# Splitting of the dense network's weights begun one attention step later, with the same order of steps

## The chip, the cores and the metric

The kernel runs on one core of a Trainium2 chip. The metric is the device time of one execution in microseconds (us), the median of three runs. The engines are named PE (matrix multiply; PEld is its weight load), DVE (vector), ACT (scalar), POOL (GpSimd) and SP, which here only issues transfers.

## The reference

Three stages follow one another: windowed attention with some global queries, a dense two-layer network, and a routed network with eight experts. Cut to its core:

```
out_g = softmax(scale * q_g @ k_all.T) @ v_all            # 32 global queries a head
out_l = softmax(mask(scale * q_l @ [k_g, k_l].T)) @ [v_g, v_l]   # |distance| <= 32
x = concat(out_g, out_l) as [1088, 512]
g = maximum(x @ w_in, 0) ** 2                             # w_in 512x2048, float64
x = g @ w_out                                             # w_out 2048x512, float64
e, gate = argmax(softmax(x @ w_gate)), its probability
out = gate * (maximum(x @ w1[e], 0) @ w2[e])              # 8 experts, with a capacity
```

## The kernel before

Attention works on 8 pairs of heads and batches. A loop over `u` from 0 to 20 runs it as a software pipeline; I call one pass an attention step, and `u4` is the pass with u = 4. A string, `ORDER`, sets what a step issues: the scores of half a pair (`S0`, `S1`: products on PE at L123, the mask and a running minimum on DVE at L127, the exponential on ACT at L130), the normalisation of the step before (`N`: DVE L134 and L135, POOL L138 and L140), the transposes of step u-2 (`T`: PE L147 and L151, copied out by DVE L148 and ACT L152), the products with the values of step u-3 (`V0`, `V1`: PE L165 and L168) and their copy (`X`: ACT L175). Every fourth step adds the global queries: `GS` (PE L186, L189) and `GX` at u = 3, 7, 11, 15; `GN` (DVE L206 to L208), `GT` (PE L215, L218; DVE L219; ACT L216) and `GV` (PE L232) in the three steps after. Every engine runs its instructions in the order in which they were written, so an instruction that waits holds up all behind it.

The keys `kd`, queries `qb` and values `vw` of a pair come by transfers that SP issues in the order of the strings `START` and `NEXT`, at the end (`L`) of every second step. The global queries `qg` of the second batch are issued behind the pair loads of u9 and are first read by `GS` at u11. SP too issues in order, and each issue can wait: for a buffer that is still in use, and for an earlier transfer that used the same completion counter.

The dense network's weights are float64. They are cut into 16 units (two halves of each 512-row or 512-column piece; 1 MB each). A unit is loaded into one of three buffers `ws` (SP, L315) and is then split on the core into two fp32r tiles in five steps: `last` (DVE L359), `sign` (DVE L364), `rebase` (ACT L367), `clamp` (DVE L372) and `join` (DVE L375). What is left of a unit rides in the steps of the next: its `high` (ACT L336, whi) in that unit's `sign`, and its `low` (DVE L339, wlo) in that unit's `rebase`, directly followed by the load of a further unit into the buffer that has come free. So units 0, 1 and 2 are loaded by the strings, and the load of unit 3 hangs on step 8 of the whole sequence, unit 4 on step 13, unit 5 on step 18, unit 6 on step 23, unit 7 on step 28.

In attention the table `EARLY` says, for each u, how many of these steps are run at five fillers, `f0` to `f4`, of `ORDER`: it places 28 steps, by ones, at `f0` (behind `N`) and `f2` (behind `S1`). The other 52 follow in the dense network, at the rate that the tables `RATE` set. That network then works in three chunks of tokens (512, 256, 320): L533 to L535 and L553 to L555 on PE, its inputs x split by ACT L511 and DVE L514. The experts come last.

Of the kernel before, what the change touches and what calls it, by code (L numbers as in the profile page):

```python
# [28 lines left out]

SPLIT = [s for u in (16, 17, 18, 19) for s in ((u, 4), (u + 1, 2))]  # L30

EARLY = [[0] * 5] * 2 + [[1, 0, 1, 0, 0]] * 12 + [[0, 0, 1, 0, 0]] * 4 + [[0] * 5] * 4
RATE = [[2, 2]] * 8 + [[2, 3]] * 4 + [[0, 0]] * 4
RATE2 = [[0, 0]] * 8 + [[2, 3], [2, 2]] * 4
NST = 3
# [369 lines left out]
def attention_moe_kernel(ctx, tc, qb, kd, vw, qg, vg, w_in, w_out, w_gate, w_gate_t, w1, w2, capacity, out):  # L405
# [24 lines left out]
    def filler(u, part):  # L430
        if u < 0:
            W.prefetch(part)
        else:
            W.run(EARLY[u][part])
        for v, p in SPLIT:
# [684 lines left out]
```

## Time and profile before

| | us |
|---|---|
| median of 3 runs (lowest to highest) | 465.28 (464.47 to 466.68) |
| the profiled execution | 462.7 |
| span of its trace | 461.0 |
| first product of attention / of the dense network on PE | 3.86 / 85.56 |
| clock of PE, mean granted | 0.988 |

The trace shows one execution. Its times count from the start of its span; 1.7 us of the profiled execution's time lie outside the span. The granted clock of PE is given as a share of 2.4 GHz, so 0.50 is the level of 1.2 GHz.

### The profile page before, as it was taken

To read this page: it belongs to the slowest core of one execution; us is meant where nothing else is said; L and a number is where in the kernel's file an instruction comes from. 1 tells how busy PE (TensorE), PEld (TensorE's weight loads), DVE (VectorE), ACT (ScalarE), POOL (GpSimd) and SP (SyncE) were. 2 spreads that over 40 slices of the span, in tenths; PEclk is the share of its full clock that TensorE was granted. 3 is DMA by queue.
4 is the path that set the end of the run, shared out by engine and by line. 5 is a ranking of instruction groups with operands and counts; after the bars stand their busy time and mean duration, and the time that the engine had idled before them with its cause. 6 is when DMAs were issued, how large, how long until landed. Compare 5 with 4: busy or idle time off the path is not lost. (4 is left out here: it accounts for less than half of the span.)

```text
span 461.0 us, 8010 instructions
## 1 busy us (share of the span) xinstructions
PE 432.4 (94%) x2963; PEld 368.8 (80%) x2963; DVE 315.8 (69%) x690; ACT 249.1 (54%) x488; POOL 79.4 (17%) x106
## 2 busy tenths in 40 slices
PE   5799999999999999999999999799999999999992
PEld 4677777888887889899999999677787777877970
DVE  3598987588799627974598688466974888647200
ACT  4587876576777734222533393156755777356210
POOL 3265636000000000000000000403202512051010
PEclk9899999999999999999999999899999999999998
DMA  8958952325254421005010468485992899711010
GB/s 250 399 182 316 326 196 94 96 91 182 97 186 176 169 104 48 24 1 194 25 46 1 146 254 332 122 257 208 306 305 95 309 349 366 298 52 41 1 39 21
DMA packets 24601, 77.26 MB, mean 168 GB/s; under 512 B 3689, under 2 KB 4841, under 8 KB 24288
## 3 DMA queue, kind: packets, MB, share of 16 engines
q1 hardware_dynamic: 19456, 64.38, 38.7%
q0 software_dynamic: 2384, 6.78, 4.9%
q10 hardware_dynamic: 2704, 5.37, 3.2%
q8 instruction: 32, 0.52, 0.5%
q14 instruction: 25, 0.20, 0.1%
HBM read 70.08 MB, written 7.41 MB: 168 GB/s over the span
## 5 line engine op out<-in xcount | busy, mean ns | idle before, releaser
L339 DVE TENSOR_TENSOR wlo<-ws,whi 128x1024 fp32r<-128x1024 f32 x80 | 94.6, 1219 | 11.5 <-ACT whi L336 10.5
L336 ACT CAST whi<-ws 128x1024 fp32r<-128x1024 f32 x80 | 83.0, 1075 | 19.2 <-DVE ws L375 10.3
L554 PE MATMUL y<-gl,whi 128*128 128x512 f32 (+2 forms) x192 | 63.2, 329 | 1.6 <-DVE gl L545 1.6
L533 PE MATMUL h<-xh,whi 128*128 128x512 f32 (+2 forms) x192 | 63.8, 332 | 0.6 <-ACT r L539 0.6
L535 PE MATMUL h<-xh,wlo 128*128 128x512 f32 (+2 forms) x192 | 62.9, 328 | 0.2 <-DVE wlo L339 0.2
L553 PE MATMUL y<-gh,whi 128*128 128x512 f32 (+2 forms) x192 | 62.9, 327 | 0.0
L534 PE MATMUL h<-xl,whi 128*128 128x512 f32 (+2 forms) x192 | 62.8, 327 | 0.0
L555 PE MATMUL y<-gh,wlo 128*128 128x512 f32 (+2 forms) x192 | 62.8, 327 | 0.0
L539 ACT ACTIVATE r<-h 128x512 f32<-128x512 f32 (+2 forms) x48 | 22.5, 470 | 42.8 <-PE h L535 35.7
L554 PEld LDWEIGHTS y<-gl,whi 128*128 128x128 f32 x192 | 36.3, 189 | 4.8 <-DVE gl L545 2.3
L533 PEld LDWEIGHTS h<-xh,whi 128*128 128x128 f32 x192 | 36.3, 189 | 3.4 <-ACT r L539 0.9
L535 PEld LDWEIGHTS h<-xh,wlo 128*128 128x128 f32 x192 | 36.3, 189 | 3.1 <-DVE wlo L339 0.6
L534 PEld LDWEIGHTS h<-xl,whi 128*128 128x128 f32 x192 | 36.3, 189 | 2.5
L545 DVE TENSOR_TENSOR gl<-r,gh 128x512 fp32r<-128x512 f32 (+2 forms) x48 | 25.7, 536 | 18.4 <-ACT r L542 15.5
L553 PEld LDWEIGHTS y<-gh,whi 128*128 128x128 f32 x192 | 36.3, 189 | 2.5
L555 PEld LDWEIGHTS y<-gh,wlo 128*128 128x128 f32 x192 | 36.3, 189 | 2.5
L130 ACT ACTIVATE P<-P,mn 128x160 f32<-128x160 f32 x64 | 27.0, 427 | 16.4 <-DVE mn L127 14.1
L583 DVE CUSTOM_DVE_ANT_0 junk<-yr,ws 128x512 bf16<-128x512 f32 x48 | 33.1, 690 | 1.2
L123 PE MATMUL s<-kd,qb 128*128 128x160 f32 x128 | 26.7, 343 | 5.2 <-DMA qb<-qb 5.2
L904 PE MATMUL bank_o<-whi,hh 128*128 128x512 f32 x72 | 29.9, 415 | 0.0
L870 POOL DMA_INDIRECT out_dram<-os,sidx x11 | 12.6, 1145 | 97.1 <-ACT os L866 96.5
L905 PE MATMUL bank_o<-wlo,hh 128*128 128x512 f32 x72 | 28.3, 393 | 0.0
(205 smaller groups left out, 895.0 us busy)
## 6 DMA issues: line engine op xcount, KB each, us to landing
ws<-w SPq DMA_DIRECT2D x62, 512.0 KB
ws<-w_in SPq DMA_DIRECT2D x8, 1024.0 KB
ws<-w_out SPq DMA_DIRECT2D x8, 1024.0 KB
vw<-vw SPq DMA_DIRECT2D x8, 512.0 KB
qb<-qb SPq DMA_DIRECT2D x7, 512.0 KB
kd<-kd SPq DMA_DIRECT2D x7, 416.0 KB
ws<-w_gate_t SPq DMA_DIRECT2D x2, 1024.0 KB
out_dram<-yr ACTq DMA_DIRECT2D x1, 2048.0 KB
```

Source lines behind the costliest of these rows:

```text
L130: nc.scalar.activation(out=P[:, a], in_=P[:, a], func=AF.Exp, bias=mn[:, a:a + 1], scale=-1.0, accum_out=su[:, a:a + 1])
L336: self.nc.scalar.copy(d["h"], f)
L339: self.nc.vector.tensor_tensor(out=d["l"], in0=f, in1=d["h"].bitcast(F32), op=ALU.subtract)
L533: nc.tensor.matmul(h, lhsT=whi[:, k, fs], rhs=xh[k], start=(k == 0), stop=False)
L534: nc.tensor.matmul(h, lhsT=whi[:, k, fs], rhs=xl[k], start=False, stop=False)
L535: nc.tensor.matmul(h, lhsT=wlo[:, k, fs], rhs=xh[k], start=False, stop=(k == 3))
L553: nc.tensor.matmul(ys[d][:, 0:gh.shape[1]], lhsT=whi[:, f % 4, ds_], rhs=gh, start=(f == 0), stop=False)
L554: nc.tensor.matmul(ys[d][:, 0:gh.shape[1]], lhsT=whi[:, f % 4, ds_], rhs=gl, start=False, stop=False)
L555: nc.tensor.matmul(ys[d][:, 0:gh.shape[1]], lhsT=wlo[:, f % 4, ds_], rhs=gh, start=False, stop=(f == 15))
L583: nc.vector.tensor_tensor_reduce(out=junk, in0=yr, in1=wgb[e], scale=1.0, scalar=0.0, op0=ALU.mult, op1=ALU.add, accum_out=L[:, i, e:e + 1])
L904: nc.tensor.matmul(o, lhsT=hh[:, k], rhs=wh[:, k % 4], start=(k == 0), stop=False)
L905: nc.tensor.matmul(o, lhsT=hh[:, k], rhs=wl[:, k % 4], start=False, stop=False)
```

## The change

```
-EARLY = [[0] * 5] * 2 + [[1, 0, 1, 0, 0]] * 12 + [[0, 0, 1, 0, 0]] * 4 + [[0] * 5] * 4
+EARLY = [[0] * 5] * 3 + [[1, 0, 1, 0, 0]] * 12 + [[0, 0, 1, 0, 0]] * 4 + [[0] * 5] * 3
```

The two splitting steps of u2 to u13, and the one of u14 to u17, become those of u3 to u14 and u15 to u18. The 28 steps, their order and the fillers within an attention step stay, and so does all that is issued after attention. Loads of units move with the steps that issue them.

DVE at u2, before (su is the softmax sum, tp the transposed weights in PSUM, PT their copy, ws a unit's buffer, s the scores):

```order
L134 TENSOR_SCALAR su<-su 128x4
L135 RECIPROCAL su<-su 128x4
L359 TENSOR_SCALAR ws<-ws 128x1024
L148 COPY PT<-tp_239 128x128
L127 ISA P,mn<-s,mask 128x160
```

The same place now:

```order
L134 TENSOR_SCALAR su<-su 128x4
L135 RECIPROCAL su<-su 128x4
L148 COPY PT<-tp_238 128x128
L127 ISA P,mn<-s,mask 128x160
L127 ISA mn 128x1
```

And DVE one step on, at u3, now:

```order
L134 TENSOR_SCALAR su<-su 128x4
L135 RECIPROCAL su<-su 128x4
L359 TENSOR_SCALAR ws<-ws 128x1024
L148 COPY PT<-tp_282 128x128
L127 ISA P,mn<-s,mask 128x160
```

The first touch of unit 0, L359, has moved from ahead of u2's copy and second scores to ahead of u3's.

SP from the loads of u3 on (- is before, + is now): kd, qb and vw are a pair's keys, queries and values, ws<-w_out is unit 3.

```order
 L75 DMA qb<-qb 128x1024
 L80 DMA vw<-vw 128x1024
-L315 DMA ws<-w_out 128x2x1024
 L74 DMA kd<-kd 128x832
 L75 DMA qb<-qb 128x1024
 L80 DMA vw<-vw 128x1024
+L315 DMA ws<-w_out 128x2x1024
 L74 DMA kd<-kd 128x832
 L75 DMA qb<-qb 128x1024
```

The load of unit 3 has moved from ahead of the loads of pair 4 to behind them. The loads of units 4 and 5 keep their places among SP's issues; that of unit 6 moves behind the last values.

DVE at u8, before, where ws_212 is the buffer of unit 1, which the load of unit 4 takes over:

```order
L134 TENSOR_SCALAR su_544<-su_544 128x4
L135 RECIPROCAL su_544<-su_544 128x4
L339 TENSOR_TENSOR wlo_408<-ws_212,whi_407 128x1024
L206 SCALAR_TENSOR_TENSOR nbg_596<-sg__597 128x1
L207 RECIPROCAL nbg_596<-nbg_596 128x1
L208 TENSOR_SCALAR Pg_588<-Pg_588,nbg_596 128x544
L148 COPY PT_659<-tp2_660 128x128
```

DVE now, from the end of u8 to u9:

```order
L364 SCALAR_TENSOR_TENSOR ws_323<-ws_323 128x1024
L127 ISA P_681,mn_682<-s_684,mask_133 128x160
L127 ISA mn_682 128x1
L127 ISA P_681,mn_682<-s_684,mask_133 128x160
L127 ISA mn_682 128x1
L134 TENSOR_SCALAR su_625<-su_625 128x4
L135 RECIPROCAL su_625<-su_625 128x4
L339 TENSOR_TENSOR wlo_476<-ws_212,whi_475 128x1024
L148 COPY PT_711<-tp2_712 128x128
```

The last reader of unit 1's buffer has moved from `f0` of u8 to `f0` of u9, and with it the moment from which SP may issue the load of unit 4.

## Rows read from the trace of the kernel before

**Rows 1.** Windows view: stretch; length, busy us (instructions) of PE, PEld, DVE, ACT, POOL; PE's clock, DMA share, GB/s.

```profile
22.35:40.61 18.26, 17.62 (x238) 14.19 (x234) 16.25 (x61) 14.60 (x48) 11.55 (x12) 1.00 0.70 268
...
88.00:160.00 72.00, 71.79 (x317) 59.12 (x316) 61.02 (x71) 49.03 (x64) 0.00 (x0) 1.00 0.40 137
```

**Rows 2.** Timeline of DVE at u2: start, duration, engine, line, [idle before, releaser].

```profile
15.59 0.69 DVE L359 TENSOR_SCALAR ws<-ws 128x1024 int32<-128x1024 int32 x1 [3.22 <-DMA ws<-w_in]
16.20 0.28 DVE L148 COPY PT<-tp 128x128 f32<-128x128 f32 x1
```

**Rows 3.** Timeline of PE from u3 to u4.

```profile
13.87 0.34 PE L165 MATMUL o<-PT,vw 128*64 128x64 f32 x4
...
16.54 0.48 PE L168 MATMUL o<-PT,vgz 128*64 128x64 f32 x4 [2.34 <-DVE PT L148]
...
19.54 1.88 PE L186 MATMUL sg<-kd,qg 128*128 128x512 f32 x4
...
22.35 0.81 PE L123 MATMUL s<-kd,qb 128*128 128x160 f32 x4
23.09 0.34 PE L165 MATMUL o<-PT,vw 128*64 128x64 f32 x4
23.26 0.29 PE L168 MATMUL o<-PT,vgz 128*64 128x64 f32 x4
...
24.95 0.34 PE L165 MATMUL o<-PT,vw 128*64 128x64 f32 x4
```

**Rows 4.** Windows view at u2 to u4, columns as in rows 1.

```profile
12.66:16.07 3.41, 1.54 (x14) 1.23 (x12) 0.48 (x1) 0.73 (x3) 1.40 (x3) 1.00 1.04 410
16.08:19.48 3.40, 2.94 (x21) 2.82 (x22) 2.95 (x14) 1.97 (x9) 0.45 (x2) 0.50 1.03 411
...
15.60:22.30 6.70, 5.76 (x45) 4.60 (x45) 5.51 (x22) 4.20 (x14) 1.54 (x3) 0.75 1.02 408
```

**Rows 5.** Page, DMA issues: number of issues and KB of each.

```profile
ws<-w_in SPq DMA_DIRECT2D x8, 1024.0 KB
...
vw<-vw SPq DMA_DIRECT2D x8, 512.0 KB
qb<-qb SPq DMA_DIRECT2D x7, 512.0 KB
kd<-kd SPq DMA_DIRECT2D x7, 416.0 KB
...
qg<-qg SPq DMA_DIRECT2D x2, 256.0 KB
```

**Rows 6.** Timeline of PE where it waits later in attention, u5 to u13.

```profile
29.86 0.31 PE L218 MATMUL tg<-ident,Pg 128*96 128x128 f32 x1 [0.17 <-DVE PT L148]
...
32.05 0.66 PE L151 MATMUL tp<-ident,Pw 128*128 128x128 f32 x4 [0.43 <-POOL Pw L140]
...
55.98 1.98 PE L186 MATMUL sg<-kd,qg 128*128 128x512 f32 x4 [0.31 <-DMA qg<-qg]
...
66.41 0.32 PE L218 MATMUL tg<-ident,Pg 128*96 128x128 f32 x1 [0.43 <-DVE PT L148]
...
67.55 0.34 PE L165 MATMUL o<-PT,vw 128*64 128x64 f32 x4 [0.26 <-ACT PT L152]
```

**Rows 7.** Timeline of SP: the issues of unit 4 and of the second qg.

```profile
45.72 0.39 SPq L315 DMA_DIRECT2D ws<-w_in  x1
...
47.97 0.59 SPq L84 DMA_DIRECT2D qg<-qg  x1
```

**Rows 8.** Timeline of DVE at the first filler of u8 and of u9.

```profile
42.35 1.20 DVE L339 TENSOR_TENSOR wlo<-ws,whi 128x1024 fp32r<-128x1024 f32 x1
...
46.66 1.20 DVE L375 SCALAR_TENSOR_TENSOR ws<-ws 128x1024 int32<-128x1024 int32 x1
```

**Rows 9.** Timeline of PE in routing, and windows view behind it.

```profile
291.07 1.23 PE L703 MATMUL lg<-Bt,A 128*128 128x72 f32 x6 [1.47 <-DVE Bt L670]
...
292.57:295.97 3.40, 3.40 (x11) 2.72 (x9) 1.62 (x9) 0.00 (x0) 2.17 (x2) 0.50 0.11 33
```

## The prediction

> **What bounds the kernel now.** I read the windows first, to see who is busy where the change acts, then the timelines of DVE, PE and SP at its places, engine by engine. In the dense network PE is the bound: 71.79 us busy of 72 [rows 1]. So if its first product comes later by some time, the kernel does too, as long as the weights keep ahead, and behind attention the change moves no step. In attention from u4 to u8 PE is busy 17.62 of 18.26 us, DVE 16.25 [rows 1]: PE again, with DVE close behind. Ahead of u4 it is different. There DVE stood idle 3.22 us for the first unit of weights, behind its su rows, and reached the small copy PT, which u0's value products need, only at 16.20 [rows 2]. PE waited 2.34 us for that copy [rows 3]. So what is to be found out is how long PE stands still in attention, before and now.
>
> **What the move takes away.** At u2 no splitting step stands ahead of PT any more. The copy can follow the su work (the wait ended at 15.59 and was 3.22 long, so it began near 12.4), and the 2.34 us wait of PE goes. L359 now stands at u3, where DVE would arrive near 15.0 (estimated: 12.4 plus the copy, two pairs of score work and N, some 2.6 us); it still waits about 0.6 us, and little hangs on that.
>
> What is late next is the keys and queries of pair 2, which S0 of u4 needs. Unit 0 landed at 15.59 [rows 2]. Behind it in SP's order come qg, unit 1, kd and qb: 256 + 1024 + 416 + 512 = 2208 KB [rows 5], 2.26 MB. The transfers ran full at 408 GB/s [rows 4], so qb lands 5.5 us later, near 21.1. PE could be there before that. From V0 at 13.87 [rows 3], V0, T and S1 take 1.86 (23.09 to 24.95 [rows 3]), so GS stands ready at 15.7 and waits for qg (256 KB behind unit 0, 0.64 us) until 16.2; GS and V1 take 2.81 (19.54 to 22.35 [rows 3]), hence 19.0. PE then stands idle 2.1 us and starts S0 of u4 at 21.1 instead of 22.35: **1.2 us earlier**, not 3.2. Between u4 and u8 two stalls of 0.17 and 0.43 us [rows 6] lie behind DVE and POOL, and DVE is now two steps less far with the splitting, so I let both go: the lead is 1.8 us at u8 (1.2 if they stay). These loads are issued unchanged, so neither end moves them.
>
> The load of unit 3 no longer stands ahead of pair 4's loads on SP. They had not made PE wait, so that part I cost at nothing; the cover is the three attention steps from u5 to u8 (the four from u4 take 18.26 us [rows 1]).
>
> **What the move adds.** The load of unit 4 is issued when L339 has read unit 1's buffer. Before, L339 ran at u8, from 42.35 for 1.2 us [rows 8], well before the issue at 45.72 [rows 7]: SP was held by its own earlier transfers. Now L339 stands at the first filler of u9, where the row of before has another step at 46.66, 1.20 us long [rows 8]. That gives an end at 47.9 in the old time, and I add 0.2 because unit 1's high on ACT now stands just one filler ahead of it: 48.1. With a lead of 1.8 it ends at 46.3, **0.6 us later** than 45.72 in spite of the lead. SP queues behind it, in order, the loads of pair 6, values, and the second qg, for which GS of u11 waits. That wait is already the end of a transfer chain: unit 4 issued at 45.72, GS released at 55.98 after 0.31 us of idling [rows 6, 7], 10.26 us in all. So GS now starts near 46.3 + 10.26 = 56.6, 0.6 us behind the old time, and the lead of 1.8 us has turned into a PE wait: without it PE would be there at 55.67 - 1.8, plus about 0.5 that I allow for u9's copies, which now stand behind L339, so near 54.4; it waits 2.2 us. Bounds for this term: if DVE reaches L339 a whole step (1.2 us) earlier, GS starts at 55.4, 0.6 ahead of before; if the lead is only 1.2, at 57.2, 1.2 behind.
>
> From u12 on the later units' loads keep enough distance: unit 5's goes from u10 to u11, with u14 as its first reader behind. At u13 a lighter step (L359 for L339) now stands ahead of the copies for which PE waited 0.43 and 0.26 us [rows 6]; I count **0.5 us gained** (0 to 0.7). At u18 one more step of about 1.2 us stands on ACT and on DVE. The same work is gone from u16 and both engines have idle time there, so I count nothing; without that cover it would cost up to 1.2.
>
> **PE's clock.** After the 2.34 us wait the granted clock stood at 0.50 from 16.08 to 19.48 [rows 4]: 1.2 GHz. The work from L168 at 16.54 to GS at 19.54 took 3.0 us, the same work at full clock 1.7 (23.26 to 24.95 [rows 3]): 1.3 us lost. It fell once more behind a wait of 1.47 us at 291.07 [rows 9], and not behind those of rows 6, up to 0.43. The new wait of 2.1 us ahead of u4 is nearest to the first, so I take one fall there, at 1.3 us. Before, that loss lay ahead of 22.35 and under the transfer of pair 2; now it lies behind 21.1, on the path. The bounds are 0 and, with the chip slow for as long as in rows 4, half of 3.4, or 1.7. The Trainium skill (TensorE: Matmul & The Clock Gate, HAM oscillation) says that waits for transfers between bursts of products can throttle PE again, but speaks of longer gaps than these; by that the sum below would be 1.3 us smaller, 465.4. This case's trace differs, at 2.34 and at 1.47 us.
>
> **Sum.** GS of u11 0.6 later, one fall 1.3, u13 -0.5: +1.4 us. The profiled execution goes from 462.7 to 464.1. The median of the runs shown lies 2.6 above it, so the median goes from 465.28 to **466.7**. A difference under 0.5% (2.3 us) is about what a measurement of this kernel can't tell from none.
>
> **Rivals.**
> - *The clock falls at both waits.* For it: the wait at u11 (2.2 us) is as long as the one that lowered it. Against: its length rests on two estimates. Another 1.3: 468.0, up to 469 at 1.7 each.
> - *It falls at neither.* For it: a wait of 2.1 has no row of its own. 465.4.
> - *The lead is kept (faster).* If the load of unit 4 is issued earlier than 45.72 less the lead, or the chain to qg is shorter than 10.26 us, PE does not wait at u11. For it: the chain of before began beside small transfers. Against: L339 cannot run before N of u9, and that needs u8's scores. The price is the whole lead: 1.8 + 0.5 less than before, 463.0 without a fall and 464.3 with one. It decides from an issue at 43.9 on, or from a chain 2.2 us shorter. The Trainium skill (DMA: Bandwidth & Descriptors, Anatomy of one DMA) fits a transfer with 2.0 us plus bytes over 436 GB/s; unit 4 to qg are 2720 KB [rows 5], 8.4 us by an estimate from that page. It would put the median at 464.8, and row 45.72 to 55.98 speaks against it.
> - *DVE and ACT pile up at the end of attention*, where u14 to u18 now carry 0.7 to 1.2 us more splitting: on top of the forecast up to 2.4, 469.1.
>
> **Chances.** One fall, as forecast: 0.40 (its own range 465.4 to 467.9). Both: 0.22. Neither: 0.15. Lead kept: 0.15. Pile-up: 0.05; none of these 0.03. Slower by over 0.5% means over 467.6: most of the second, the pile-up and the upper end of the first, 0.31. Faster by over 0.5% means under 462.95: about half of the kept lead, 0.08. Within: 0.61. The range of 463.7 to 468.8 leaves out half of the kept lead, the dear end of two falls, and most of the pile-up.
>
> **What would show it.** In the profile of the changed kernel: DVE without its 3.22 us idle at u2; PE idle some 2 us ahead of u4's first score, released by qb near 21.1; the load of unit 4 issued near 46 to 48; GS of u11 released by qg some 10 us later, after a PE wait of about 2 us; one stretch, or two, at clock 0.50 behind these waits; first product of the dense network near 87.0 instead of 85.56. It is wrong if GS of u11 has no wait for qg, if u4 starts well before 21, or if PE loses time behind u14.

## The result, and the profile after

| | before | after |
|---|---|---|
| median of the runs compared (lowest to highest), us | 464.22 (461.1 to 469.36), 20 runs | 466.6 (464.3 to 470.94), 20 runs |
| ratio of the runs, 95% interval | | 1.0062 (1.0035 to 1.0089) |
| the profiled execution, its span, us | 462.7, 461.0 | 469.16, 467.4 |
| first product of the dense network, us | 85.56 | 88.51 |

The change makes the kernel 0.6% slower, some 2.4 to 2.9 us. The forecast time, 466.7, is 0.1 from the measured one, but the forecast difference was 1.4 us: the median of the first three runs of before, from which I counted, lay 1 us above that of the 20. The two profiled executions are 6.4 us apart, more than the medians, and only 2.95 of it has arisen by the first dense product. So one pair of traces is not enough here; more executions of the same two kernels follow among the experiments. Ratios leave out executions more than 1.5% above the fastest of their kernel, the medians in us do not, so a ratio can differ from the quotient of two medians.

At the start, the timeline of DVE shows PT copied at 12.48 with no splitting step ahead of it, and L359 a step later, waiting 0.90 us where it waited 3.22 [rows 2]:

```profile
12.48 0.26 DVE L148 COPY PT<-tp 128x128 f32<-128x128 f32 x1
15.79 0.77 DVE L359 TENSOR_SCALAR ws<-ws 128x1024 int32<-128x1024 int32 x1 [0.90 <-DMA ws<-w_in]
```

The timeline of PE no longer has the wait for PT [rows 3]. In its place stand a wait of 2.00 us for the queries of pair 2 at S0 of u4, one of 2.31 us for qg at GS of u11, where 0.31 was [rows 6], and two small ones in u9 and u10:

```profile
16.46 1.98 PE L186 MATMUL sg<-kd,qg 128*128 128x512 f32 x4 [0.91 <-DMA qg<-qg]
21.45 1.36 PE L123 MATMUL s<-kd,qb 128*128 128x160 f32 x4 [2.00 <-DMA qb<-qb]
...
47.44 0.31 PE L218 MATMUL tg<-ident,Pg 128*96 128x128 f32 x1 [0.44 <-DVE PT L148]
48.59 0.34 PE L165 MATMUL o<-PT,vw 128*64 128x64 f32 x4 [0.27 <-ACT PT L152]
57.79 2.57 PE L186 MATMUL sg<-kd,qg 128*128 128x512 f32 x4 [2.31 <-DMA qg<-qg]
...
88.51 0.50 PE L533 MATMUL h<-xh,whi 128*128 128x512 f32 x1
```

The timelines of DVE and SP show the chain that ends in the second wait. L339, the last reader of unit 1's buffer, runs 3.63 us later than before [rows 8]; unit 4's load is issued right behind it, 1.49 us later than before [rows 7], and qg behind that:

```profile
45.98 1.20 DVE L339 TENSOR_TENSOR wlo<-ws,whi 128x1024 fp32r<-128x1024 f32 x1
```

```profile
47.21 0.39 SPq L315 DMA_DIRECT2D ws<-w_in  x1
48.16 0.42 SPq L75 DMA_DIRECT2D qb<-qb  x1
49.40 0.60 SPq L84 DMA_DIRECT2D qg<-qg  x1
```

From the issue to GS it is 10.58 us (10.26 before). The windows view, with the columns of rows 1, shows the clock at 0.50, which is 1.2 GHz, behind both waits, and for 13.65 us in routing, where before had 3.40 [rows 9]. The dense network is PE's as before [rows 1]:

```profile
21.50:24.91 3.41, 3.41 (x25) 2.96 (x26) 1.84 (x10) 1.53 (x5) 0.92 (x2) 0.50 1.02 406
59.05:62.46 3.41, 3.41 (x23) 2.41 (x22) 1.10 (x3) 0.75 (x3) 0.00 (x0) 0.50 0.92 339
88.60:160.00 71.40, 71.23 (x313) 58.64 (x314) 61.13 (x73) 48.74 (x65) 0.00 (x0) 1.00 0.44 148
291.15:304.80 13.65, 12.27 (x50) 9.32 (x48) 4.88 (x25) 1.55 (x5) 4.67 (x5) 0.50 0.40 120
```

### The profile page after: what moved, and what is told of

Read it like the earlier page. It is cut to its first block, busy times and chain, and to the rows that moved or that the text cites. A ratio compares the mean times of both kernels' runs of the same rounds, so it can differ in the third digit from the quotient of the medians.

```text
span 467.4 us, 8009 instructions
## 1 busy us (share of the span) xinstructions
PE 436.5 (93%) x2963; PEld 371.5 (79%) x2963; DVE 316.6 (68%) x690; ACT 249.5 (53%) x488; POOL 79.4 (17%) x106
## 5 line engine op out<-in xcount | busy, mean ns | idle before, releaser
L339 DVE TENSOR_TENSOR wlo<-ws,whi 128x1024 fp32r<-128x1024 f32 x80 | 94.7, 1221 | 11.6 <-ACT whi L336 10.5
L127 DVE CUSTOM_DVE_ANT_0 P<-s,mask 128x160 f32<-128x160 f32 x64 | 18.1, 319 | 15.5 <-PE s L123 15.2
```

Of the source, the lines that this page charges most:

```text
L339: self.nc.vector.tensor_tensor(out=d["l"], in0=f, in1=d["h"].bitcast(F32), op=ALU.subtract)
```

## The experiments

My theory: the later release of unit 1's buffer moves unit 4's load, qg queues behind that load on SP, and the clock falls behind the new waits. The rivals: the added steps at u14 to u18; the clock alone; the wait at u4.

**qg ahead of unit 4's load.** The changed kernel with the second batch's qg issued with the loads of u7:

```
-NEXT = ["w1 k2 v1", "w1 k3 v2", "k4 v3", "k5 v4 h0 h1", "k6 v5 g1 h2", "k7 v6 h3", "v7"]
+NEXT = ["w1 k2 v1", "w1 k3 v2", "k4 v3", "k5 v4 g1 h0 h1", "k6 v5 h2", "k7 v6 h3", "v7"]
```

> The changed kernel with one load moved: the second batch's qg is issued behind pair 5's values (u7) instead of behind pair 6's (u9), so it no longer queues behind the load of unit 4. Order theory (GS of u11 is late because qg queues behind unit 4, whose issue hangs on u9's splitting step; half clock follows that wait): the 2.3 us wait of PE ahead of GS of u11 goes and with it the half-clock stretch behind it; the first product of the dense network comes near 84.7 us instead of 88.5 in the changed kernel and 85.6 before; time near 462.6, below the kernel before. Rival (the loss comes from the splitting steps that now lie in u14 to u18): nothing changes there, dense network from 88.5, time as the changed kernel, 466.6.

Measured: 462.28 us, ratio to before 0.9921 (0.9886 to 0.9956). PE and SP, by their timelines:

```profile
21.41 0.91 PE L123 MATMUL s<-kd,qb 128*128 128x160 f32 x4 [2.00 <-DMA qb<-qb]
55.26 1.88 PE L186 MATMUL sg<-kd,qg 128*128 128x512 f32 x4
66.62 0.78 PE L123 MATMUL s<-kd,qb 128*128 128x160 f32 x4 [1.25 <-DMA qb<-qb]
```

```profile
47.15 0.39 SPq L315 DMA_DIRECT2D ws<-w_in  x1
```

Unit 4 is issued as late as in the changed kernel (47.15 against 47.21), so the splitting is as late, and all of the added work of u14 to u18 is there. But GS of u11 starts 2.53 us earlier, without a wait, and the first dense product comes at 85.16 instead of 88.51 (87.30 and 87.63 in two further executions of the changed kernel, below). What the change cost at u11 was the place of qg in SP's queue. The late steps cost nothing that shows. A next transfer is exposed at once: pair 7's queries, 1.25 us. They stand behind unit 5's load, issued at 57.63 (57.69 in the changed kernel), and PE now reaches them earlier. Against the kernel before, this execution has gained nothing by the first dense product (85.16 against 85.21 in the mean of three), so where the 0.8% over that kernel comes from is not shown.

**The steps caught up.** The changed kernel with two steps at each filler of u3, so that from u4 on the splitting stands where it stood before:

```
-EARLY = [[0] * 5] * 3 + [[1, 0, 1, 0, 0]] * 12 + [[0, 0, 1, 0, 0]] * 4 + [[0] * 5] * 3
+EARLY = [[0] * 5] * 3 + [[2, 0, 2, 0, 0]] + [[1, 0, 1, 0, 0]] * 10 + [[0, 0, 1, 0, 0]] * 4 + [[0] * 5] * 4
```

> The kernel before with the four steps of u2 and u3 all run at u3 (two at each filler), so that splitting begins one attention step later but is back on the old schedule from u4. Order theory: the wait for qb ahead of u4's first score (2.0 us, to about 21.4) and its half-clock stretch stay; unit 4 is issued near 45.7 as before, GS of u11 waits about 1 us for qg; dense network from about 85.5, time as before (464, within 0.5%). Rival (what costs is beginning later at all): as slow as the changed kernel, 466.6.

Measured: 463.09 us, ratio 0.9965 (0.993 to 1.0). The timelines of PE and SP:

```profile
21.44 0.78 PE L123 MATMUL s<-kd,qb 128*128 128x160 f32 x4 [1.98 <-DMA qb<-qb]
54.58 1.98 PE L186 MATMUL sg<-kd,qg 128*128 128x512 f32 x4
```

```profile
44.57 0.39 SPq L315 DMA_DIRECT2D ws<-w_in  x1
46.77 0.60 SPq L84 DMA_DIRECT2D qg<-qg  x1
```

The wait for pair 2 is that of the changed kernel, and here no stretch at half clock follows it. Unit 4 is issued 1.15 us earlier than in the first execution of before (0.19 earlier than in its second, below), and no wait for qg of the 1 us that I had expected comes: qg follows within 2.20 us, and GS starts 10.01 behind unit 4. The first dense product comes at 84.13, where I had given 85.5. With the first step late and the rest on time the kernel is no slower than before.

**The late release alone.** The first steps at u2 as before, u6 left without steps, so that from u7 on the splitting is as late as in the changed kernel:

```
-EARLY = [[0] * 5] * 3 + [[1, 0, 1, 0, 0]] * 12 + [[0, 0, 1, 0, 0]] * 4 + [[0] * 5] * 3
+EARLY = [[0] * 5] * 2 + [[1, 0, 1, 0, 0]] * 4 + [[0] * 5] + [[1, 0, 1, 0, 0]] * 8 + [[0, 0, 1, 0, 0]] * 4 + [[0] * 5] * 3
```

> The kernel before with the gap put in at u6: steps 1 to 8 stay where they were, all later ones come one attention step later, as in the changed kernel. Order theory: DVE keeps its 3.2 us wait at u2, unit 4 is issued near 48, PE waits about 2.7 us for qg ahead of GS of u11, a half-clock stretch follows; dense network from about 89, time about 467.8, slower than before by 0.6 to 0.9%. Rival (the loss comes from the beginning of attention, u2 to u4): no slower than before, dense network from 85.6.

Measured: 467.9 us, ratio 1.0062 (1.0023 to 1.0101), the whole loss of the change without its first part. The timeline of PE has the old wait at u3 and the new one at u11; the windows behind both are at full clock in this execution:

```profile
17.56 0.34 PE L168 MATMUL o<-PT,vgz 128*64 128x64 f32 x4 [2.58 <-DVE PT L148]
58.26 1.98 PE L186 MATMUL sg<-kd,qg 128*128 128x512 f32 x4 [2.21 <-DMA qg<-qg]
```

```profile
18.70:22.20 3.50, 3.40 (x30) 2.23 (x28) 2.56 (x14) 2.74 (x9) 1.54 (x3) 1.00 1.03 410
58.30:61.70 3.40, 3.40 (x28) 2.31 (x28) 1.00 (x3) 1.10 (x2) 0.41 (x1) 1.00 0.66 189
```

So neither a wait of 2.58 us nor one of 2.21 us always lowers the clock. Unit 4 is issued at 47.78, as late as in the changed kernel. I had expected a fall and the first dense product near 89; it came at 87.44.

**PE kept busy in the waits.** The changed kernel with products added that nothing needs, written over by the real scores: six ahead of S0 of u4, seven ahead of `GS` of u11 (the third, g = 2). The cut leaves out arguments of the calls.

```
+            if (u, j2) == (4, 0):
+                for _ in range(6): matmul(s[:, 0], lhsT=ident, rhs=ld["k", 1][:, 0:160])
...
+        if g == 2:
+            for _ in range(7): matmul(s[:, 0:160], lhsT=ident, rhs=ld["k", 5][:, 0:160])
```

> The changed kernel with products on PE that nobody reads in its two waits: six ahead of u4's first score (about 1.9 us) and seven ahead of GS of u11 (about 2.2 us), into PSUM that the real products then overwrite. Clock theory (each wait costs its length, and the half-clock stretch behind it another 1.3 to 1.7 us): both waits for transfers stay where they are in time, but clock 0.50 no longer follows them; dense network from about 85.3, time about 463.4, some 3 us under the changed kernel. Rival (the waits alone cost, the clock nothing): dense network from 88.5, time 466.6 or more.

Measured: 464.24 us, ratio 0.9979 (0.9941 to 1.0016). The windows view has full clock up to the first dense product at 85.14:

```profile
13.79:85.00 71.21, 68.43 (x930) 55.87 (x928) 59.21 (x211) 53.76 (x172) 35.45 (x53) 1.00 0.62 233
```

The timeline of PE has S0 of u4 and of u8, and GS of u11 (its lines are numbered a few higher here):

```profile
20.86 0.78 PE L126 MATMUL s<-kd,qb 128*128 128x160 f32 x4
...
38.19 0.81 PE L126 MATMUL s<-kd,qb 128*128 128x160 f32 x4
...
55.97 1.98 PE L192 MATMUL sg<-kd,qg 128*128 128x512 f32 x4 [0.31 <-DMA qg<-qg]
```

The table and the transfers are those of the changed kernel and only the waits are filled, yet its ratio is 0.8% lower. With no fall behind u4, unit 4 was issued at 45.48 and GS of u11 started 1.8 us earlier than in the changed kernel. From S0 of u4 to that of u8 it takes 17.33 us; the changed kernel with its fall takes 18.46, so the fall costs some 1.1 us there. That the clock stayed up because of the products is argued and not shown by this trace: five other executions under the profiler have no fall in attention and no such products (the second of before, the second and third experiment, and two below). For it speak the ratio and the mean clock of the twelve executions, 0.984 against 0.979 in the changed kernel.

**qg early in the kernel before.** The same edit of `NEXT` as in the first experiment, on before:

> The kernel before with the second batch's qg loaded one attention step earlier (with pair 6's keys, ahead of unit 4's load). Order theory: qg matters only where it is waited for, and before it was waited for 0.31 us at GS of u11; so GS there starts 0.3 us earlier without a wait, the first dense product near 85.3, ratio to before 0.997 to 1.001 (same). Rival, that an earlier qg is worth something by itself whatever the table says: ratio 0.992 as in the change with qg early, dense network near 82.6.

Measured: 463.83 us, ratio 1.0002 (0.9967 to 1.0037). The timeline of PE has GS of u11 without a wait:

```profile
54.68 1.88 PE L186 MATMUL sg<-kd,qg 128*128 128x512 f32 x4
```

The first dense product comes at 84.12, in an execution that had no fall in attention; an execution of before without one has 55.11 and 84.67 (below). So before the change qg's place was worth about half a microsecond in these traces and nothing that the runs can tell from none, as forecast; after it, 2.5 us.

**Pair 2 ahead of unit 1.** The changed kernel with

```
-NEXT = ["w1 k2 v1", "w1 k3 v2", "k4 v3", "k5 v4 h0 h1", "k6 v5 g1 h2", "k7 v6 h3", "v7"]
+NEXT = ["k2 v1 w1", "w1 k3 v2", "k4 v3", "k5 v4 h0 h1", "k6 v5 g1 h2", "k7 v6 h3", "v7"]
```

> The changed kernel with pair 2's keys and queries and pair 1's values loaded ahead of unit 1; qg stays behind unit 4. That takes away the wait of 2.0 us at u4: S0 of u4 near 19.4 instead of 21.45, no stretch at half clock there. Theory that the load of unit 4 and the transfers queued behind it set the rest: unit 4's issue hangs on DVE and moves by 1 to 2 us at most (45.2 to 46.5), so GS of u11 starts near 56.3 after a wait for qg of 2.5 to 4, and the first dense product comes near 87 (86 to 87.5): about 2 us of the gain at u4 do not come out, ratio 0.997 to 1.004. Rival, that the wait at u4 was the cost of the change: dense network near 85 or earlier with no wait of over 1.5 us at u11, ratio near 0.993.

Measured: 465.64 us, ratio 1.0053 (1.0016 to 1.0089). S0 of u4 starts at 18.20, but the timeline of PE shows where the 3.25 us go:

```profile
27.71 1.40 PE L123 MATMUL s<-kd,qb 128*128 128x160 f32 x4 [2.32 <-DMA qb<-qb]
...
57.08 2.55 PE L186 MATMUL sg<-kd,qg 128*128 128x512 f32 x4 [2.31 <-DMA qg<-qg]
```

The wait has gone to pair 3 at u6, and the one for qg stands as it was; the first dense product comes at 87.82, after a fall behind each. The wait at u4 was not the cost of the change. The ratio is 0.1% above what I gave, and GS of u11 and the first dense product are 0.8 us later.

**Both.** The two edits of `NEXT` together on the changed kernel, and the same with the steps caught up at u3:

> The changed kernel with both: pair 2 ahead of unit 1 and qg ahead of unit 4. Both waits of the change go. Theory: S0 of u4 near 19.4, GS of u11 near 53.3 to 54 without a wait, first dense product 83.2 if pair 7's queries keep up, 84.5 to 85.2 if the wait for them at u14 (1.25 us with qg alone moved) grows by the lead. Ratio to before 0.987 to 0.993. Rival, that DVE and not the transfers limits attention from u4 on: dense network stays at 85.2 and the lead is used up in waits for DVE or ACT before u11.

> As the run before, with the splitting begun at u3 but caught up there (two steps at each of the two fillers), so that units 3 to 6 are loaded when they were loaded in the kernel before. Theory: unit 4 issued near 43.5 and unit 5 early enough that pair 7's queries are not waited for; dense network at 82.5 to 83.5; ratio 0.985 to 0.992. Rival: the two extra steps at u3 lie on the path to u4, since no wait hides them any longer; dense network near 84.5 to 85, ratio 0.993 to 0.997.

Measured: 461.95 us, ratio 0.9954 (0.9916 to 0.9992), first dense product at 84.78; and 462.83 us, ratio 0.9999 (0.9956 to 1.0042), 83.69. Both ratios are higher than expected, and GS of u11 is later in the former (55.69 for 53.3 to 54). By the medians of all executions the latter is 0.35% faster than before (462.83 against 464.45). The timelines of PE, first of the former, then of the latter:

```profile
28.75 1.38 PE L123 MATMUL s<-kd,qb 128*128 128x160 f32 x4 [2.53 <-DMA qb<-qb]
55.69 1.88 PE L186 MATMUL sg<-kd,qg 128*128 128x512 f32 x4
66.11 0.78 PE L123 MATMUL s<-kd,qb 128*128 128x160 f32 x4 [0.31 <-DMA qb<-qb]
```

```profile
22.67 0.81 PE L123 MATMUL s<-kd,qb 128*128 128x160 f32 x4 [0.94 <-DVE mn L127]
...
54.23 1.88 PE L186 MATMUL sg<-kd,qg 128*128 128x512 f32 x4
```

In the former the lead of u4 is spent at u6 on pair 3; in the latter, where DVE has two more splitting steps at u3, PE waits 0.94 us for DVE at the second scores of u4. The first experiment's kernel and the former of these two beat both kernels of the study; their intervals overlap.

**The two kernels again.** Is the 6.4 us between the profiled executions the change's? Each kernel was profiled twice more.

> The changed kernel as it is, once more under the profiler. Theory: what the table of steps sets comes back to within 0.3 us (L359 at u3 near 15.8, S0 of u4 near 21.4 after a wait of 2.0 for pair 2, unit 4 issued near 45.5 to 47.2, GS of u11 about 10.5 us behind that issue after a wait of 2 or more); what the clock does varies: none, one or both falls in attention, so the first dense product between 85.9 and 88.6, and 3.4 to 17 us at half clock in routing; from the first dense product to the end 375.3 to 376.1 us with 3.4 us there, 377.3 to 377.6 with 10.2, 378.4 to 379.1 with 13.65 or 17. Rival: the two falls and the 13.65 us in routing belong to the changed kernel and come back, first dense product 88.5, span 467.4.

> The same once more: by the theory the waits as in the first look, the clock again by its own; by the rival 88.5 and 467.4 again.

> The kernel before, once more under the profiler. Theory: the wait of 2.3 to 2.7 us for the copy PT at u3 and the unit 4 to GS of u11 chain come back; the fall behind that wait may come or not, first dense product 84.3 to 85.6; half clock in routing 3.4 to 17 us as in the changed kernel, and the part behind the first dense product by its length as said there. Rival: one fall and 3.4 us in routing again, 85.56 and 461.0.

> The same once more: by the theory the waits as in the first look, the clock by its own; by the rival 85.56 and 461.0 again.

Measured, from the timelines of PE and SP of the three executions each (the first of each is the one shown above). The first row lies ahead of all that the change moves:

| us | before | after |
|---|---|---|
| unit 0 issued | 8.00, 8.22, 8.18 | 8.17, 8.41, 8.69 |
| S0 of u4 | 22.35, 21.47, 22.44 | 21.45, 21.83, 22.13 |
| S0 of u8 | 40.61, 39.69, 40.69 | 39.91, 40.30, 40.59 |
| unit 4 issued | 45.72, 44.76, 45.72 | 47.21, 47.58, 47.87 |
| GS of u11 | 55.98, 55.11, 55.86 | 57.79, 58.11, 58.44 |
| GS of u15 | 74.30, 73.43, 74.17 | 77.16, 75.94, 76.26 |
| first dense product | 85.56, 84.67, 85.40 | 88.51, 87.30, 87.63 |
| from there to the end of the span | 375.4, 378.5, 379.5 | 378.9, 378.9, 376.6 |
| falls of the clock to 0.50 in attention | 1, 0, 1 | 2, 1, 1 |

The second execution of before has the wait for PT without a fall behind it (timeline of PE, and windows view):

```profile
16.76 0.34 PE L168 MATMUL o<-PT,vgz 128*64 128x64 f32 x4 [2.62 <-DVE PT L148]
...
21.47 0.78 PE L123 MATMUL s<-kd,qb 128*128 128x160 f32 x4 [0.17 <-DVE ws L372]
```

```profile
16.80:20.20 3.40, 3.40 (x27) 2.38 (x27) 2.94 (x16) 2.46 (x9) 0.95 (x3) 1.00 1.02 406
```

The windows view at half clock in routing, the further executions of after and then of before; the second of these four has two falls in its stretch with full clock between them:

```profile
289.51:299.74 10.23, 9.22 (x44) 7.62 (x42) 4.85 (x24) 1.84 (x4) 3.38 (x4) 0.50 0.32 104
```

```profile
289.42:299.66 10.24, 8.95 (x47) 7.58 (x47) 5.37 (x27) 1.87 (x4) 2.78 (x3) 0.67 0.35 114
```

```profile
285.38:299.03 13.65, 12.64 (x58) 10.87 (x58) 5.70 (x29) 1.88 (x4) 3.73 (x4) 0.50 0.39 135
```

```profile
286.20:299.85 13.65, 12.64 (x58) 10.86 (x58) 5.70 (x29) 1.87 (x4) 3.72 (x4) 0.50 0.38 132
```

The waits came back; of the clock's stretches in attention only the one behind u4 came back each time. Unit 0 is issued 0.29 us later in the mean of after, ahead of any difference between the kernels, so that much of every later difference in the table is the executions' own. Behind the first dense product the two kernels take the same on the mean, 377.8 and 378.1 us, and before has the 13.65 us in routing as well. So the 3.45 us that the first pair of executions differs by there are not the change's. The rival, that they belong to the changed kernel, falls. Several numbers of the theory missed: S0 of u4 (21.83 and 22.13 for 21.4) and the issue of unit 4 (47.58 and 47.87 for 47.2 at the latest) in after, the wait for PT in the third execution of before (1.84 us for 2.3 to 2.7), and behind the first dense product 378.9 us with 10.2 at half clock (377.3 to 377.6 given) and 379.5 with 13.65 (379.1 at most).

**All executions together.** For 191 executions the mean granted clock is recorded (73 of before, 22 of after, 12 of each of the first eight experiments; for the 20 of before in the result it is not). I fitted one straight line of time against clock through them, with one height for each kernel: the slope is 0.29 us for 0.001 of the clock, and 0.76 us of scatter is left of a spread of up to 9 us within a kernel. The heights, at a clock of 0.985 (standard error 0.1 to 0.2): before 463.64, after 465.15; late release alone 466.4, pair 2 first 464.9, PE kept busy 464.1, before with qg early 463.4, caught up with both 463.1, caught up 463.0, qg first 462.5, both 461.9. So at equal clock the change costs 1.5 us. The plain means of these executions, 464.9 and 466.9, are 2.0 apart, and the other 0.5 is a lower clock (0.9806 and 0.9790 on the mean): no execution of after was above 0.987, and 8 of the 73 of before were at 0.991. The late release alone costs 2.7 us at equal clock, so the other part of the change gives back some 1.2. The first experiment's kernel is 1.2 us below before at equal clock, and a higher clock (0.985 on the mean) goes with the rest of its gain.

## Why the prediction came out, point by point

- *The wait for PT goes, and L359 waits little at u3*: shown (0.90 us; 0.6 forecast).
- *Pair 2's queries are late next*: shown, released at 21.45 after 2.00 us (21.1 after 2.1 forecast).
- *A lead of 1.2 us at u4 and 1.8 at u8*: **this step failed.** In the mean of three executions the lead is 0.3 us at u4 (22.09 against 21.80; 0.6 if counted from the issue of unit 0) and 0.1 at u8. I had taken the start of S0 in before, 22.35, from an execution with a fall at 16.08 and held that loss to be hidden under the transfer of pair 2. It was not: where the same kernel had no fall behind the same wait, S0 started at 21.47, and that is where the wait for pair 2 holds it in the changed kernel. So against an execution of before without a fall the removed stall was worth nothing ahead of u4: what I had counted as the lead was the loss by that execution's fall. From u4 to u8 the small stalls do go, as forecast, for 0.9 us (17.33 in the fourth experiment against 18.24 before; 0.6 forecast), and the fall behind u4 takes 1.1 of it back (18.46; 1.3 forecast, at the end of the sum).
- *Unit 4 is issued 0.6 us later*: with the forecast fall that means 46.3 + 1.3, or 47.6, and 47.21 to 47.87 were measured. In the mean of three the issue moves by 2.15 us, for the lead is missing and before's first execution was one of the two late ones.
- *GS of u11 follows 10.26 us behind*: shown, 10.53 to 10.58, with PE waits of 2.26 to 2.31 (2.2 forecast). In the mean GS starts 2.46 us later; the sum had 0.6 + 1.3 = 1.9. The rival's 8.4 us are an estimate by the Trainium skill (DMA: Bandwidth & Descriptors, Anatomy of one DMA); that section gives its fit for transfers that GpSimd issues, and here SP issues them. By it the wait at u11 would have been 1.9 us shorter. The trace differs, with 10.14 to 10.58 us in the six executions.
- *The clock*: one fall as forecast in two executions of three, both in one. The second cost 1.5 us: from GS to the first dense product 30.72 us with it, 29.19 without. All three had the one behind u4. The Trainium skill (TensorE: Matmul & The Clock Gate, HAM oscillation) speaks of longer gaps than these; the trace differs in the falls behind 2.00 and 2.31 us, and agrees in the second and third experiment, where waits of 1.98 to 2.58 us had none.
- *u13 gains 0.5 us*: shown. From GS of u11 to GS of u15 18.32 us before, in the mean, and 17.83 after without a fall.
- *The added steps at u18 cost nothing, the pile-up is a rival*: nearly so. From GS of u15 to the dense network 11.24 us before and 11.36 after, in the mean of three: 0.1 us.
- *The sum*: +2.46 for GS, +0.5 for a fall of 1.5 us in one execution of three, -0.4 for u13 and u18, is +2.6, the difference of the first dense products (87.81 against 85.21), where I had +1.4. Two terms were short: GS of u11, by the lead, and a second fall, which the sum left out. That the absolute time agrees to 0.1 us is luck: the forecast difference was 1 us too small, and the median of before from which I counted 1 us too high. The direction and both waits came out; the largest chance stood on "within 0.5%", and the measurement, 0.62%, lies just beyond it.

What stays open is what decides whether a given wait is followed by a fall: the same wait had one in one execution and none in another. Over all executions under the profiler, the wait for pair 2 at u4 was followed by one in 4 of 5, that for qg at u11 in 2 of 5, that for PT in 2 of 5.

## What to carry to other kernels

When work is moved, look for the transfers that hang on it and for all that is queued behind them on the issuing engine: here a quarter-megabyte load behind a one-megabyte load made PE wait 2.3 us, and putting it ahead of that load turned a loss of 0.6% into a gain of 0.8%. Removing a stall exposes the next transfer in the queue, so the gain is bounded by when that one lands; moving pair 2's transfers ahead only handed the wait on to pair 3. Take the state that a term rests on from several executions: a row behind a stretch at half clock is late by its own accident.

## What the hardware showed that I had not expected

The granted clock varies from one execution to the next of the same kernel (0.968 to 0.991 for the kernel before), and goes with most of the spread of its times, 0.29 us for each 0.001. In routing PE was at 1.2 GHz for 3.4 us in one execution of before and for 13.65 us in two others, although it was busy 12.64 of the 13.65. With the PE waits filled by useless products, attention ran from 13.79 to 85 us at full clock in the one execution profiled, and the ratio fell from 1.0062 to 0.9979: the products cost less than the idling that they replaced.
